# A two-layer recurrent-memory transformer on one core: the instruction order planned anew, one unit's product tied to VectorE, one row load released earlier

## The chip, the cores and the metric

The kernel runs on one core of one Trainium2 chip. The core has five engines that run side by side, each with its own queue of instructions: TensorE (PE, with its weight loads shown apart as PEld), VectorE (DVE), ScalarE (ACT), GpSimd (POOL) and SyncE (SP, which here only issues DMAs). The metric is the device time in microseconds of one execution. The times before are the median of three runs. The profile is of one further execution, whose own time is given beside its span.

## The reference

The input is one sequence of 2048 rows of 512 values in bf16. Two blocks, A and B, are applied twice, each on a normalised input and added back:

```python
    x = A_x
    x = x + _A_ref(_layernorm(x, axis=-1), A_mem0, A_Wq, A_Wk, A_Wv, A_Wo, A_seg_len)
    x = x + _B_ref(_layernorm(x, axis=-1), B_w1, B_w2)
    x = x + _A_ref(_layernorm(x, axis=-1), A_mem0, A_Wq, A_Wk, A_Wv, A_Wo, A_seg_len)
    x = x + _B_ref(_layernorm(x, axis=-1), B_w1, B_w2)
```

A is attention over segments of 32 rows with 8 memory rows in front, 32 heads of 128. The memory rows that a segment gives are the next segment's memory, so the 64 segments follow one another:

```python
        for s in range(n_seg):
            xs = x[:, s * seg_len:(s + 1) * seg_len, :].copy()
            h = jnp.concatenate([mem, xs], axis=1)
            q = jnp.einsum('btd,dhe->bhte', h, Wq)
            k = jnp.einsum('btd,dhe->bhte', h, Wk)
            v = jnp.einsum('btd,dhe->bhte', h, Wv)
            scores = jnp.einsum('bhqe,bhke->bhqk', q, k) * scale
            scores = jnp.where(mask[None, None], scores, -1000000000.0)
            p = _softmax(scores, axis=-1)
            o = jnp.einsum('bhqk,bhke->bhqe', p, v)
            o = jnp.einsum('bhte,hed->btd', o, Wo)
            mem = o[:, :M, :].copy()
            outs.append(o[:, M:, :])
```

B is a dense layer, relu(x w1) w2 with an inner width of 1376. The weights of A and of B are the same in both applications.

## The kernel before

The work goes in 66 steps. Step k handles segment k of the first application and segment k-2 of the second one together ("two layers" a = 0 and 1, 40 columns each: 32 rows and 8 memory rows). Steps 0 and 1 have the first layer alone, steps 64 and 65 the second alone. All weights stay in SBUF.

One step consists of these operations, whose names also stand in the planning tables:

- `queries_keys`: q and k projections from HT (the transposed 40 + 40 columns), 16 matmuls for four heads, copied out of PSUM to qT and kT by ACT or DVE.
- `values.mm.0` to `.3`: the value projection, copied to vw; some DMAs then place parts of vw in V0 (`place_values`, on SP).
- five units, `u0` to `u4`. Units 0 and 1 (`BLOCKED`) and unit 2 have eight heads, units 3 and 4 four heads. For each: `scores.mm` on TensorE; then on DVE `block` (adds the mask), `top` (maximum), `sub`; `exp` on ACT; on DVE `total` and `recip`; then `mul`. In units 0 and 1 `mul` and a 32-by-32 transpose (`turn`) are on DVE, and four copies, `stay` and `shift` for two halves, on ACT or POOL bring the result to PT. In units 2 to 4 `mul` may be on POOL or DVE, `turn` is on TensorE, and two masked copies (`keep`) bring it to PM.
- `attend`: probabilities times values, copied to OT by ACT or DVE (`attend.ev`).
- `project.mm.0` to `.4`: the output product from OT, one for each unit, accumulated in one PSUM bank (`st`). From it `project.ev` copies the new memory columns into the next step's HT (this is the recurrence: the next step's projections wait for it) and `project.rows` the others to OX.
- `finish`: OX is transposed by a DMA on SP (`finish.turn`), added to x on DVE (`add`), normalised over halves (`layernorm_halves`, "da"), turned on TensorE (`turned.turn.da`), and goes through the dense layer (`dense_layer.mm.da.0` to `.5`, with `relu` on ACT or DVE). The sum with the dense result (`total_x`) is normalised again ("db": `stats`, `swap`, `aggr` on DVE or ACT, `rstd.power` on POOL, `norm` on DVE), turned (`turned.turn.db`) and copied to the second layer's columns of the HT of the step after next. POOL also does `narrow`, `carry` (for the rows to be stored and the next x) and `widen` (the rows of the step after next from bf16 to f32).
- every fourth step `load_group` loads the next 128 rows by SP (`xb`, L919), normalises them ("dl") and turns them by a DMA.
- in steps 5 to 54 `late_values` computes value rows for later groups, one or two products a step.

The first 57 us load the weights (Wv, Wq, Wk, Wo on POOL's queue, w1 and w2 on SP's), spin TensorE on zeros, and compute value rows for seven row groups (`*values.mmg1.0` and so on).

Nothing of the order stands in the code as such. Class `Plan` collects all operations with their reads and writes, an engine or a choice of two engines, and a cost in microseconds for each. `order` then places them one after another in a planned time: on TensorE in the order of `PLACE` (a number for each product and phase of the run, plus `PERIOD` for each step), on other engines by a priority that follows from the operations that come after, shifted by the table `AHEAD`; `LOOK` is how far it looks past the earliest start. Where an operation may run on two engines, it is given to the one that ends it earlier in the planned time. `PAIRED` names products that take over the 64-column mode of the product before them. The instructions are then issued in the order of their planned starts, each engine's queue in that order. So a cost that is changed in the code changes nothing in an instruction itself, but can change the order on all engines and the engine of an operation.

Lines to know: L742 all 128-column and 64-column products by `across`, L1029 and L1031 copies by ACT and by DVE, L1035 and L1037 those of units 0 and 1 by ACT and by POOL, L1223 `sub`, L1226 `exp`, L1229 `total`, L1248 `mul` of units 2 to 4, L796 `norm` over halves, L765 statistics of whole rows, L747 and L752 the two parts of `rstd.power`, L919 the load of xb, L562 and L567 the loads of w1 and w2, L965 the transpose of OX.

Of the kernel before, what the change touches and what calls it, by code (L numbers as in the profile page):

```python
# [30 lines left out]
LOOK = 0.1074729  # L31
PERIOD = 26.155362
PLACE = {
# [421 lines left out]
def kernel(  # L455
# [21 lines left out]
    L = M + SEG  # L477
# [18 lines left out]
    plan = Plan()  # L496
# [994 lines left out]
```

## Time and profile before

| | us |
|---|---|
| median of three runs | 1590.68 (1589.81 to 1591.3) |
| time of the profiled execution | 1592.36 |
| its span | 1590.6 |
| start to the end of step 0's output products | 57.07 |
| step 1 | 25.71 |
| step 2 | 25.17 |
| step 3 | 25.08 |
| steps 4 to 63, each | 22.9 to 24.1 |
| step 63's end to the end of the span | 47.96 |

The mean granted clock of TensorE is 0.997 of full speed over the span. The chain of waits, which follows the work back from the last instruction, gives 90% of the span to TensorE, 3% to ScalarE, 2% to VectorE and 1% each to GpSimd and to DMAs. GpSimd waits 408.5 us for VectorE's second normalisation statistics (L793) in 64 waits, and VectorE 292.5 us for the DMA transpose of OX in 65 waits; both have little else to do at that point of a step. In the table of waits TensorE's own longest entries are small, 3.8 us for the copies to HT in 13 waits and 3.0 us for copies of hT in two.

In a timeline, a row is one instruction or several equal ones (xN), with its start and its length, and in brackets how long its engine had stood idle and what ended that. A matmul's length is from its issue to its modelled end, about 0.2 us, while matmuls follow each other at 0.036 us (128 columns, 80 rows).

### The profile page before, as it was taken

To read this page: it belongs to the slowest core of one execution; us is meant where nothing else is said; L and a number is where in the kernel's file an instruction comes from. 1 tells how busy PE (TensorE), PEld (TensorE's weight loads), DVE (VectorE), ACT (ScalarE), POOL (GpSimd) and SP (SyncE) were. 2 spreads that over 40 slices of the span, in tenths; PEclk is the share of its full clock that TensorE was granted. 3 is DMA by queue.
4 is the path that set the end of the run, shared out by engine and by line. 5 is a ranking of instruction groups with operands and counts; after the bars stand their busy time and mean duration, and the time that the engine had idled before them with its cause. 6 is when DMAs were issued, how large, how long until landed. Compare 5 with 4: busy or idle time off the path is not lost.

```text
span 1590.6 us, 101922 instructions
## 1 busy us (share of the span) xinstructions
PE 1566.3 (98%) x45454; PEld 1403.1 (88%) x45454; DVE 1024.2 (64%) x3237; ACT 1177.5 (74%) x3189; POOL 516.1 (32%) x1384
## 2 busy tenths in 40 slices
PE   8999999999999999999999999999999999999998
PEld 5688899889989989988988998999898998898887
DVE  4566766766765766676676576666667567667665
ACT  4567777777777777777777777777777777777775
POOL 5133323323323322332332333333233233233221
PEclk9999999999999999999999999999999999999999
DMA  9711111111011111111111111111011111110100
GB/s 371 241 38 26 26 27 32 28 25 40 21 37 28 31 28 24 29 33 34 26 33 23 33 25 38 34 24 35 21 31 28 27 32 26 26 26 21 25 17 8
DMA packets 67080, 66.74 MB, mean 42 GB/s; under 512 B 43496, under 2 KB 52944, under 8 KB 66640
## 3 DMA queue, kind: packets, MB, share of 16 engines
q1 hardware_dynamic: 60624, 39.89, 11.3%
q0 software_dynamic: 4992, 19.40, 3.2%
q8 instruction: 356, 5.83, 1.6%
q10 hardware_dynamic: 1024, 0.93, 0.2%
q14 instruction: 84, 0.69, 0.2%
HBM read 31.53 MB, written 9.96 MB: 26 GB/s over the span
## 4 chain that ended last, share of the span: by engine, by line
PE 90%; ACT 3%; DVE 2%; issue 1%; POOL 1%; DMA 1%; SPq 0%; POOLq 0%; DVEq 0%; ACTq 0%
PE work L742 36%; PE st L742 19%; PE fill L1101 16%; PE fill L742 7%; PE work L1332 5%; PE fill L864 5%; PE work L1190 3%; ACT PT L1035 1%; ACT es L1226 1%; DMA V<-vw 1%; ACT kT L1029 0%; DMA xb<-in_A_x_dram 0%; DVE es L1223 0%; ACT hT L852 0%; DVE mx L1213 0%
## 5 line engine op out<-in xcount | busy, mean ns | idle before, releaser
L742 PE MATMUL work<-HT,Wq_sb 128*128 128x80 bf16 (+2 forms) x10400 | 373.1, 201 | 3.9 <-ACT HT L1029 3.5
L742 PE MATMUL work<-HT,Wk_sb 128*128 128x80 bf16 (+2 forms) x10400 | 362.4, 201 | 0.7 <-ACT HT L1029 0.4
L742 PEld LDWEIGHTS <-Wq_sb 128*128 128x128 bf16 (+1 forms) x10400 | 334.2, 104 | 22.8 <-issue 5.7
L742 PE MATMUL st<-OT,Wo_sb 128*128 128x80 bf16 (+1 forms) x8448 | 344.6, 201 | 0.2 <-ACT OT L1029 0.2
L742 PEld LDWEIGHTS <-Wk_sb 128*128 128x128 bf16 (+1 forms) x10400 | 328.7, 104 | 14.2 <-issue 1.2
L742 PEld LDWEIGHTS <-Wo_sb 128*128 128x128 bf16 x8448 | 319.5, 99 | 16.3 <-issue 13.3
L1101 PE MATMUL fill<-Wv_sb,HT 128*64 128x512 bf16 x2112 | 274.7, 382 | 3.3 <-ACT hT L852 3.0
L1037 POOL COPY PT<-es 32x32 f32<-32x32 f32 (+4 forms) x521 | 156.1, 300 | 350.7 <-PE work L1190 164.3
L1029 ACT CAST qT<-work 128x320 bf16<-128x320 f32 (+1 forms) x452 | 188.8, 418 | 82.4 <-PE work L742 50.0
L1029 ACT CAST kT<-work 128x320 bf16<-128x320 f32 (+1 forms) x479 | 199.1, 416 | 42.9 <-PE work L742 4.5
L1029 ACT CAST vw<-fill 128x512 bf16<-128x512 f32 x258 | 151.2, 586 | 90.6 <-PE fill L1101 88.1
L747 POOL TENSOR_SCALAR ln<-ln 128x1 f32<-128x1 f32 x159 | 35.4, 223 | 524.2 <-DVE ln L793 408.5
L1029 ACT CAST OT<-work 128x320 bf16<-128x320 f32 (+1 forms) x399 | 152.6, 418 | 40.4 <-PE work L1332 39.3
L1270 ACT ACTIVATE PM<-work,half 128x160 bf16<-128x160 f32 (+2 forms) x317 | 133.8, 442 | 34.1 <-PE work L742 32.2
L1101 PEld LDWEIGHTS <-HT 128*64 128x64 bf16 x2112 | 101.5, 111 | 63.3 <-issue 4.8
L1223 DVE TENSOR_TENSOR es<-es,mx 128x320 f32<-128x320 f32 (+2 forms) x330 | 150.8, 469 | 1.8
L1226 ACT ACTIVATE es<-es 128x320 f32<-128x320 f32 (+2 forms) x330 | 130.3, 410 | 25.1 <-DVE es L1223 21.4
L1229 DVE TENSOR_REDUCE sm<-es 128x8 f32<-128x320 f32 (+2 forms) x330 | 128.5, 402 | 30.4 <-ACT es L1226 29.6
L1213 DVE TENSOR_REDUCE mx<-es 128x8 f32<-128x320 f32 (+2 forms) x330 | 127.6, 399 | 0.3
L742 PE MATMUL fill<-xnM,w_sb 128*128 128x64 bf16 (+1 forms) x3668 | 119.3, 194 | 0.7 <-ACT xnM L1029 0.5
L1204 DVE TENSOR_TENSOR es<-work,maskb 128x320 f32<-128x320 f32 (+1 forms) x132 | 59.0, 476 | 94.2 <-PE work L1190 91.4
L1190 PEld LDWEIGHTS <-qT 128*40 128x40 bf16 x4096 | 83.5, 98 | 33.5 <-issue 1.1
(111 smaller groups left out, 2361.0 us busy)
## 6 DMA issues: line engine op xcount, KB each, us to landing
V<-vw SPq DMA_DIRECT2D x248, 48.0 KB
V<-vh SPq DMA_DIRECT2D x120, 64.0 KB
Wq_sb<-in_A_Wq_dram POOLq DMA_DIRECT2D x2, 2048.0 KB, 23.0
Wk_sb<-in_A_Wk_dram POOLq DMA_DIRECT2D x2, 2048.0 KB, 28.1
Wo_sb<-in_A_Wo_dram POOLq DMA_DIRECT2D x2, 2048.0 KB, 39.9
vh<-vg SPq DMA_DIRECT2D x32, 128.0 KB
xb<-in_A_x_dram SPq DMA_DIRECT2D x16, 128.0 KB
Wv_sb<-in_A_Wv_dram POOLq DMA_DIRECT2D x1, 2048.0 KB, 13.3
```

Of the source, the lines that this page charges most:

```text
L742: nc.tensor.matmul(out_[u:v, :], lhsT=lhsT[:, u:v], rhs=rhs, start=start, stop=stop, tile_position=(0, u), **more)
L864: nc.tensor.matmul(yp[64 * u:64 * u + 64, 0:256], lhsT=hT[:, fc, :], rhs=w2_sb[:, fc, :].rearrange("p (j u d) -> p u j d", j=2, u=2)[:, u, ...
L1029: nc.scalar.copy(out=out_, in_=in_)
L1037: nc.gpsimd.tensor_copy(out=out_, in_=in_)
L1101: nc.tensor.matmul(vp[64 * b:64 * b + 64, :], lhsT=cols(c4), rhs=Wv_sb[:, c4, n * 512:(n + 1) * 512], start=(c4 == 0), stop=(c4 == NC4 - 1 ...
L1190: nc.tensor.matmul(v[64 * t:64 * t + L, a, i, s, :], lhsT=qT[:, hi, a * L:(a + 1) * L], rhs=kT[:, hi, a * L:(a + 1) * L], start=True, stop ...
L1213: nc.vector.tensor_reduce(out=by_head(mx), in_=e_rows(), axis=AX.X, op=ALU.max)
L1223: nc.vector.tensor_tensor(out=e_spread(), in0=e_spread(), op=ALU.subtract, in1=i1)
L1226: nc.scalar.activation(out=es[:, A], in_=es[:, A], func=ACTF.Exp, scale=SCALE)
L1229: nc.vector.tensor_reduce(out=by_head(sm), in_=e_rows(), axis=AX.X, op=ALU.add)
L1270: nc.scalar.activation(out=o, in_=i, func=ACTF.Copy, scale=half[:, b:b + 1])
L1332: nc.tensor.matmul(o[u:u + cols, :, a, :], lhsT=V[:, p, e0 + u:e0 + u + cols], rhs=spread(a, i, h2), start=True, stop=True, tile_position= ...
```

## The change

The two planning tables, `PAIRED` and `LOOK` are replaced (some 300 numbers; four lines of each are shown), and these costs and rules with them. `PERIOD` stays.

```diff
-LOOK = 0.1074729
+LOOK = 0.1164413
 PERIOD = 26.155362
 PLACE = {
-    ("*turned.turng0.0", 2): 113.397, ("*turned.turng1.0", 2): 114.607, ("*turned.turng2.0", 2): 122.366,
...
 PAIRED = {
-    ("project.mm.1", 0), ("project.mm.2", 0), ("project.mm.2", 4), ("project.mm.4", 0), ("project.mm.4", 4),
...
+    ("project.mm.1", 0), ("project.mm.2", 0), ("project.mm.3", 0), ("project.mm.4", 0), ("queries_keys.mmu0.0", 0),
...
 AHEAD = {
-    ("*layernorm.aggr", 1): -3.303, ("*layernorm.norm", 1): 34862.154, ("*layernorm.stats", 1): -2.846,
...
+    ("*layernorm.aggr", 1): -7.952, ("*layernorm.stats", 1): -189070.642, ("*make_mask", 1): 4.661,
...
 def t_moved(eng, n):
-    return 0.205 + 0.86e-3 * n if eng == ACT else 0.20 + 1.08e-3 * n
+    return 0.25 + 0.86e-3 * n if eng == ACT else 0.19 + 1.08e-3 * n
...
-            plan.op(POOL, 0.95, power, r=["half"], w=[ln])
+            plan.op(POOL, 0.82, power, r=["half"], w=[ln])
...
-        plan.op((ACT, DVE), (0.2, 0.2), swap, w=[ln])
+        plan.op((ACT, DVE), (0.30, 0.26), swap, w=[ln])
...
-        plan.op(DVE, 0.26, norm, r=[ln, *keys], w=[xn])
+        plan.op(DVE, 0.32, norm, r=[ln, *keys], w=[xn])
...
-        plan.op(SP, 0.78, load, r=[("taken", 4 * g - 4), ("out", 4 * g - 4)], w=[xb], lag=2.45)
+        plan.op(SP, 0.78, load, r=[("taken", 4 * g - 4), *([("out", 4 * g - 4)] if g > 1 else [])], w=[xb], lag=2.45)
...
-            plan.op(POOL, 2 * t_copy(256), carry, r=[("z", 0)], w=[keys[1]])
+            plan.op(POOL, 0.92, carry, r=[("z", 0)], w=[keys[1]])
...
-                plan.op(POOL, t_copy(256), narrow, r=[("z", 1)], w=[ob])
+                plan.op(POOL, 0.45, narrow, r=[("z", 1)], w=[ob])
...
-            def mul(eng):
+            def mul(eng=DVE):
...
-            plan.op((POOL, DVE), (t_pool(n), t_dve(n)), mul, r=[es, sm], w=where)
+            plan.op(*(((POOL, DVE), (t_pool(n), t_dve(n))) if n <= 160 else (DVE, t_dve(n))), mul, r=[es, sm], w=where)
...
-            plan.op((ACT, POOL), (t_moved(ACT, L * nj), t_moved(POOL, L * nj) + 0.07), stay, r=[es, PT], w=[(PT, b)])
+            plan.op((ACT, POOL), (t_moved(ACT, L * nj), t_moved(POOL, L * nj)), stay, r=[es, PT], w=[(PT, b)])
```

Two of these edits change what may be done, beside the order. `mul` of the third unit (`u2`, n = 320 in steps with both layers) can no longer go to POOL. The load of the first further row group (`load_group` with g = 1, in step 1) no longer waits for step 0's transpose of OX on SP (`("out", 0)`); it still waits for step 0's memory copy (`("taken", 0)`).

What the built programs show of the order: both have the same 10,822 planned operations. In a steady step the order on TensorE is, before and after (an excerpt from the first scores to the end of the step; pairs of `qk` stand for `queries_keys`, `da` for the dense layer, `sc` for scores, `at` for attend, `pr` for the output product):

```
before: sc1 sc0 qk2.2 v2 qk2.0 qk2.1 turn.da v1 qk2.3 v3 sc2 qk3.0 da0 qk3.1 qk4.0 qk4.1 da1 sc3 da2 sc4
        at1 at0 da3 da4 turn2 da5 pr0 turn3 at2 pr1 at3 turn4 pr2 at4 pr3 turn.db pr4
after:  sc0 sc1 qk2.0 qk2.2 v0 v1 qk2.1 qk2.3 v3 sc2 turn.da qk4.0 qk3.0 da0 qk3.1 da1 qk4.1 sc3 da2 at0
        sc4 at1 da3 turn2 da4 da5 pr0 turn3 at2 pr1 turn4 at3 pr2 at4 pr3 turn.db pr4
```

The DVE order of step 30, from unit 3's reciprocal on, and POOL's from unit 2's product on:

```
DVE  before: recip3 total_x stats.db total4 recip4 aggr.db mul4 keep3.1 norm.db at.ev3.0
     after:  recip3 total_x total4 stats.db recip4 mul4 keep3.1 swap.db aggr.db at.ev3.0 norm.db
POOL before: mul2 mul3 narrow carry rstd.db widen
     after:  mul3 narrow carry widen rstd.db
```

Engines of operations that have a choice, over the run, where many moved:

| operation | before | after |
|---|---|---|
| `scores.mul` | DVE 207, POOL 123 | DVE 267, POOL 63 |
| `layernorm_halves.swap.db` | DVE 4, ACT 60 | DVE 64 |
| `dense_layer.relu` | ACT 195, DVE 3 | ACT 148, DVE 50 |
| `queries_keys.ev` | ACT 931, DVE 125 | ACT 975, DVE 81 |
| `scores.stay` and `shift` | ACT 201, POOL 327 | ACT 152, POOL 376 |
| `scores.keep` | DVE 79, ACT 317 | DVE 57, ACT 339 |

On SP the first lines change from "transpose of OX, four w1 loads, xb load, w2 loads, row transpose" to "xb load, transpose of OX, four w1 loads, row transpose, w2 loads". On POOL the mask and the second root stand ahead of the two Wo loads; before, they stood behind.

More of the change, by code (lines that the diff above doesn't have):

```diff
@@ new lines @@
+    ("*layernorm.aggr", 1): -7.952, ("*layernorm.stats", 1): -189070.642, ("*make_mask", 1): 4.661,
+    ("*prepare_more.zero_w2", 1): -41.906, ("*rstd.raise_", 1): -5.01, ("*turned.keep", 1): 140461.982,
+    ("*turned.turn", 1): 130.17, ("attend.ev", 0): 0.205, ("attend.ev", 2): 0.149, ("attend.mm", 0): -141847.173,
+    ("attend.mm", 1): 93388.877, ("bulk.land", 1): 0.047, ("dense_layer.mm.da", 1): 0.081,
+    ("dense_layer.relu.da", 0): -75998.358, ("dense_layer.relu.da", 1): 3230.06, ("dense_layer.relu.da", 2): -0.052,
@@ new lines @@
+    ("early_store.put", 1): -49649.171, ("finish.add", 0): -35230.884, ("finish.add", 1): -12100.287,
+    ("finish.add", 2): -64.499, ("finish.narrow.db", 0): -1.52, ("finish.store.da", 2): -13.443,
+    ("finish.store.db", 0): -0.123, ("finish.total_out.da", 2): -90151.838, ("finish.total_x.da", 0): -0.024,
+    ("finish.total_x.da", 1): 0.284, ("finish.turn", 2): 33.797, ("finish.turn_near", 2): 3.087,
+    ("finish.widen", 0): 1.436, ("finish.widen", 1): 10.067, ("get_x", 1): -54690.148, ("late_values.ev", 0): -3.113,
@@ new lines @@
+    ("layernorm_halves.norm.da", 2): 0.151, ("layernorm_halves.norm.db", 0): 2.128,
+    ("layernorm_halves.norm.db", 1): -0.915, ("layernorm_halves.stats.da", 0): 13687.157,
+    ("layernorm_halves.stats.da", 1): 0.323, ("layernorm_halves.stats.da", 2): -84750.62,
+    ("layernorm_halves.stats.db", 0): -2.938, ("layernorm_halves.stats.db", 1): 1.326,
+    ("layernorm_halves.swap.da", 0): -56685.136, ("layernorm_halves.swap.da", 1): 0.655,
+    ("layernorm_halves.swap.da", 2): 36.788, ("layernorm_halves.swap.db", 0): 0.227,
@@ new lines @@
+    ("layernorm_halves.swap.db", 1): 131238.655, ("load_group.load.dl", 0): -3.193, ("load_group.load.dl", 1): -2.217,
+    ("load_group.turn_far.dl", 1): 0.841, ("load_weights.dma", 1): -23604.969, ("place_values.dma", 1): -1.747,
+    ("prep_x.cp", 0): -0.338, ("prep_x.cp", 1): -3.672, ("prepare.first_exp", 1): -19.747, ("prepare.keep", 1): 8.604,
+    ("prepare.place", 1): 53401.671, ("prepare.turn", 1): 2.221, ("prepare.zero", 1): -1354.661,
+    ("prepare.zero_last", 1): -98887.921, ("prepare.zero_none", 1): -1.096, ("prepare_late.load", 0): -92232.192,
@@ new lines @@
+    ("project.ev", 0): 0.174, ("project.ev", 1): 0.154, ("project.ev", 2): -1.945, ("project.first", 1): -69.357,
+    ("project.mm", 0): 10.274, ("project.mm", 1): 133742.033, ("project.mm", 2): 65.416,
+    ("project.rows", 0): -2766.799, ("project.rows", 1): 7.099, ("queries_keys.ev", 0): 15.868,
+    ("queries_keys.ev", 2): -103526.145, ("queries_keys.mm", 0): -70335.54, ("queries_keys.mm", 2): -1.989,
+    ("rstd.power.da", 0): 1.301, ("rstd.power.da", 1): 143.283, ("rstd.power.da", 2): -9.528,
@@ new lines @@
+    ("rstd.power.db", 0): -21571.742, ("rstd.power.dl", 1): 0.41, ("scores.block", 0): 0.227,
+    ("scores.block", 1): 1.135, ("scores.block", 2): 42546.547, ("scores.exp", 1): 3.968, ("scores.exp", 2): -22.937,
+    ("scores.keep", 1): 120278.391, ("scores.mm", 0): 0.965, ("scores.mm", 1): -0.13, ("scores.mm", 2): 53469.948,
+    ("scores.mul", 0): 112.91, ("scores.mul", 1): 0.096, ("scores.mul", 2): 12.538, ("scores.recip", 1): 52381.849,
+    ("scores.recip", 2): -3.712, ("scores.shift", 1): 28746.395, ("scores.shift", 2): 20526.276,
@@ new lines @@
+    ("scores.stay", 0): -2299.032, ("scores.stay", 2): -40540.573, ("scores.sub", 0): -37.08,
+    ("scores.sub", 1): -32755.82, ("scores.sub", 2): 1.716, ("scores.top", 0): 27715.681, ("scores.total", 1): 97.858,
+    ("scores.total", 2): 208136.995, ("scores.turn", 1): -53625.561, ("scores.turn", 2): 0.246,
+    ("turned.keep", 0): 2.548, ("turned.keep.da", 1): 44.635, ("turned.keep.da", 2): 144612.281,
+    ("turned.keep.db", 1): 185440.58, ("turned.turn", 0): -38648.799, ("turned.turn.da", 0): -75405.957,
@@ L204 @@
+    ("turned.turn.da", 2): 0.583, ("turned.turn.db", 0): -73377.416, ("values.ev", 0): 0.441, ("values.ev", 1): 0.01,
+    ("values.ev", 2): -59.755, ("values.mm", 0): -25.052, ("values.mm", 1): 35.335, ("values.mm", 2): 0.371,
+    ("zero_columns.zero", 1): -12272.977,
 }
```

54 lines of the change are left out of this document (6 added, 48 removed), and 230 rows, old and new, of tables (PAIRED, PLACE).

## The prediction

> **What bounds the kernel now.** The busy table comes first, then the stages cut at the last output product of steps 0, 1, 2, 3 and 63.
>
> ```profile
> PE 1566.3 (98%) x45454; PEld 1403.1 (88%) x45454; DVE 1024.2 (64%) x3237; ACT 1177.5 (74%) x3189; POOL 516.1 (32%) x1384
> ```
> ```profile
> 0.00:57.07 57.07, 50.95 (x801) 33.15 (x802) 26.52 (x90) 29.40 (x70) 24.10 (x63) 0.94 0.93 351
> 57.07:82.78 25.71, 21.99 (x560) 17.38 (x560) 14.18 (x57) 13.29 (x44) 7.24 (x20) 1.00 0.59 168
> ...
> 133.03:1542.64 1409.61, 1403.60 (x41564) 1273.31 (x41564) 924.16 (x2883) 1073.27 (x2889) 461.67 (x1236) 1.00 0.13 28
> ```
>
> Columns: stretch, length, busy time of PE, PEld, DVE, ACT, POOL, granted clock, DMA share, GB/s. TensorE bounds every stage, so only time in which it waits can be won. Its busy time hides short waits, because a matmul counts 0.2 us from issue to end while the next follows after 0.036 us. I therefore took, from the trace, the time from each planned product's first matmul to that of the next one, and its excess over the shortest tenth of the same product in steps 3 to 62. These excesses add up to 28 us, and 0.47 us of them in each of the nine steps from 55 on is the step's own round trip (last output product, copy, next projection). An ordinary step loses about 0.27 us: 0.08 ahead of unit 1's attend, 0.03 ahead of unit 3's turn, 0.15 ahead of the fourth output product. A step that normalises a row group (every fourth) loses about 0.45. The largest single wait is in step 1, in the chain of waits and in the timelines of DVE and PE:
>
> ```profile
> 61.70 6.23 DMA xb<-in_A_x_dram
> ```
> ```profile
> 67.94 0.69 DVE L765 BATCH_NORM_STATS2 ln<-xb 128x6 f32<-128x512 bf16 x1 [3.33 <-DMA xb<-in_A_x_dram]
> ```
> ```profile
> 71.48 1.05 PE L1101 MATMUL fill<-Wv_sb,HT 128*64 128x512 bf16 x8 [2.85 <-ACT hT L852]
> ```
>
> The row load leaves SP at 61.70, behind four weight loads (58.62 to 61.64). VectorE stands 3.33 us at its statistics, with the scores' totals queued behind them, and TensorE stands 2.85 us for the work that comes of these.
>
> Last, one ordinary step (30, whose first score product is at 749.96; times "+" count from there):
>
> ```profile
> 760.32 0.66 DVE L1223 TENSOR_TENSOR es<-es,mx 128x160 f32<-128x160 f32 x1
> ...
> 761.75 0.31 DVE L1223 TENSOR_TENSOR es<-es,mx 128x160 f32<-128x160 f32 x1
> ...
> 765.04 0.57 DVE L796 TENSOR_SCALAR xr<-vx,ln 128x256 bf16<-128x256 f32 x1 [0.85 <-POOL ln L752]
> 765.53 0.48 DVE L1031 CAST OT<-work 128x320 bf16<-128x320 f32 x1
> ```
> ```profile
> 760.07 0.72 POOL L1248 TENSOR_TENSOR P<-es,sm 128x320 bf16<-128x320 f32 x1 [0.55 <-ACT hT L852]
> 762.29 0.45 POOL L1248 TENSOR_TENSOR P<-es,sm 128x160 bf16<-128x160 f32 x1 [1.50 <-ACT PM L1270]
> ```
> ```profile
> 765.88 0.20 PE L1332 MATMUL work<-PM,vw 128*128 128x80 bf16 x1
> 766.06 0.73 PE L742 MATMUL st<-OT,Wo_sb 128*128 128x80 bf16 x16
> ```
>
> VectorE is full from +0.5 to +14. The same subtraction takes 0.31 alone and 0.66 while GpSimd multiplies. Unit 3's copy to OT stands behind a normalisation that waits 0.85 for GpSimd, and the fourth output product starts late for it (766.06).
>
> **The change, part by part.** In the changed program each steady step has the same TensorE products, the same four switches between 128 and 64 columns (0.096 each), only in another order; so TensorE's work there is unchanged and the sum is one of waits.
>
> *Steady step, worked with the rows of step 30.* DVE: unit 0's block at +0.47; two blocks, tops, subtractions at 0.40 each; normalisation; totals from +3.36 (subtraction ends 2.56, exp 2.69 to 3.16); both products and transposes end at +6.62; unit 2's subtraction at +7.51. Its exp follows on ACT at +8.14 to 8.60 (before: 8.64 to 9.10, behind three more copies), so its total starts at +8.64, 0.5 earlier. Now the third unit's product stands on DVE: 61 POOL products of 0.725 go, and 61 come to DVE. The nearest row is the one such product DVE ran before (0.493); bounds 0.44 (start to start) and 0.73. I take 0.44. In return unit 3's subtraction takes 0.31, not 0.66, and one PSUM copy fewer (0.46) stands between. A relu (the 256-column one that DVE ran took 0.43) falls into a wait for a projection. Reciprocal of unit 3 comes out at +11.95 to 12.10, against 12.02 to 12.19, POOL's product at 12.25 to 12.70, against TensorE's need at +12.82: the 0.03 may go. Unit 4's product ends at +13.9, needed at +14.33. Unit 0's attend at +9.51 needs copies that are done by +8; unit 1's at +9.9 needs a bank freed by unit 3's block at +9.8: the 0.08 goes. Unit 3's copy to OT now precedes the normalisation: DVE +14.85 to 15.3, needed at +15.83: the 0.15 goes. So 0.22 of 0.27, in 44 steps: -9.7 (bounds 0 and -11.9).
>
> *Steps with a row group.* The statistics (0.69) and the normalisation (0.40) still stand in DVE's chain: unit 3's turn comes at +13.05 against 12.82, unit 1's attend about 0.1 late. 0.45 becomes 0.25, 15 steps: -3.0 (bounds +1.5 and -6.8). Two steps stood 0.78 and 0.40 for a late row transpose (first at 1152.20); the product that waits now stands 2.6 us later in its step: -1.0.
>
> *What gets worse.* POOL's widen (0.83) now stands ahead of the second normalisation's root in 59 steps; it stood behind. And the pair of swap copies moved from ACT (60 of 64) to DVE (0.34), behind unit 4's product. DVE: aggregate ends +14.73. POOL: product to 12.70, narrow 0.40, carry 0.89, widen 0.83 end at +14.95; root 0.88 to +15.85; normalisation 0.41, no longer slowed to 0.57 by widen, to +16.29; turn possible at +16.4, and TensorE is there at +16.40. The second of before had 1.0 us to spare; this has none. In 20 steps a late value product (0.44) now stands right ahead and covers it. I take 0.06 in 40 steps: +2.5 (bounds 0 and 0.45 each, +18).
>
> *Other moved evacuations* (relu, swap, stay and shift pieces, OT copies): ACT loses net 97 operations, DVE gains 108, both inside the sums above; the cover is the slack given there.
>
> *Start.* The early rows' first turn still waits for POOL's first root (ends 7.21) behind the same transfers. After it four value products stand ahead of the second turn; two waits of before, 1.08 us at 10.07 and 0.73 at 18.13, are filled. The first product that needs the second Wv transfer (landed at 16.2 by the trace's DMA events, as the other landings here) started at 18.87, and could start at 16.4 to 17.0. The mask (2.6 us of POOL) moves ahead of the second root; this ends at 10.95 instead of 10.75, needed after 12.7. A cap: the third output product needs the last Wo transfer, landed at 50.5; it started at 55.02. So 0 to -4.3; I take -3.0. One value product (0.87) moves from step 0 into step 1, which cancels.
>
> *The row load.* It stands ahead of the output transpose on SP, can leave at about the step's start and lands while DVE waits for that transpose anyway (5.94 us idle there): -2.8 (bounds 0 and -3.7, the whole idle time of this stage). The transpose, and the four weight loads behind it, leave 0.46 later; the dense layer's turn stands nine products later in the step, which covers it (uncovered: 0.46). The second weights move behind the row transpose; they landed at 75.2 at the latest and are needed some 3 us earlier than before: bound +1. Steps 2, 3 and the tail: 0 (bounds -1.5 and +1.5).
>
> Cost constants, LOOK and the planning tables act through the order alone.
>
> Sum: -9.7 - 3.0 - 1.0 + 2.5 - 3.0 - 2.8 = -17.0. The profiled execution took 1592.36 (span 1590.6 and 1.8 around it), so 1575.4; it lies 1.7 above the median 1590.68. The forecast, as a median, is 1573.7, or **1574**.
>
> [...]
>
> **Rivals.**
> *The root comes late (slower).* One mechanism: widen ahead of the root on POOL. Unit 3's product, carry or widen each stretch when DVE is active (copies of the same shape spread from 0.31 to 0.46, the carry halves from 0.39 to 0.46). If the root starts 0.5 later than worked out, the turn stands in some 40 uncovered steps: 20 us in place of 2.5, which makes 1591; at 0.7 it is 1599. It decides from 0.49 on (19.5 over 40). For: no slack is left. Against: widen now leaves the normalisation unslowed, and the root itself stretched in few cases (0.567 median, 0.570 at the ninth tenth).
> *Waits only move.* DVE's chain is held by POOL once a step, 0.35 as the subtraction was; unit 3's and unit 4's turns then stand as long as the waits removed, and the steady gain (11.2) is gone: 1585. For: six POOL copies of units 0 and 1 now follow one another. Against: POOL's longest instruction leaves.
> *The early load is hidden anyway*: the transpose or the weights behind it hold step 1 in its place: 1576.5; with the start's gain lost too, 1580.
> *More than the forecast*: all steady waits but the round trips go (24), and the start reaches its caps (8): about 1559.
>
> **Chances.** Forecast 0.50; root late 0.20; waits only move 0.14; load hidden 0.08; more 0.08. A measurement of this kernel tells about 0.2% (3.2 us) from no change. Faster: 0.50 + 0.08 + 0.08 and 0.08 of the waits that move, 0.74; within 0.2%: the rest of these 0.06 and 0.02 of the late root, 0.08; slower: 0.18. Range 1562 to 1598, from near the lowest bound to the late root at 0.7; its own range, without the rivals, is 1565 to 1584.
>
> **What would show it.** In step 1 the statistics of xb with no DMA wait, and no TensorE gap over 1 us. In a steady step: OT's DVE copy ahead of the normalisation; no gap ahead of the fourth output product; unit 3's subtraction at 0.31; steps of 23.1 in place of 23.33. Wrong: gaps ahead of the second normalisation's turn (TensorE waiting for xr), or ahead of the turns of units 3 and 4.

## The result, and the profile after

The changed kernel takes 1577.05 us (median of 4 runs, 1576.44 to 1580.34), beside 1590.99 for the kernel before (median of 4): a ratio of 0.9917, interval 0.9900 to 0.9935, so 0.65 to 1.0% faster. The slowest of the four, 1580.34, had a mean granted clock of 0.997, the other three 1.0. The forecast was 1574. The profiled executions, against which the sum was made, took 1592.36 and 1576.44: 15.9 less, where the sum said 17.0. A later series gave 1576.58 (e11 below).

The busy table of the changed kernel, then the stages cut, as before, at the last output product of steps 0, 1, 2, 3 and 63 (stretch, length, busy time of PE, PEld, DVE, ACT, POOL, granted clock, DMA share, GB/s):

```profile
PE 1553.5 (99%) x45393; PEld 1389.3 (88%) x45393; DVE 1074.4 (68%) x3406; ACT 1126.3 (72%) x3011; POOL 479.8 (30%) x1393
```
```profile
0.00:54.13 54.13, 48.28 (x789) 32.44 (x789) 26.57 (x89) 28.63 (x68) 25.72 (x68) 1.00 0.98 370
54.13:80.04 25.91, 23.32 (x571) 17.77 (x568) 13.47 (x55) 14.15 (x46) 5.86 (x17) 1.00 0.60 186
...
105.23:128.93 23.70, 23.04 (x691) 20.85 (x692) 17.68 (x54) 16.78 (x46) 7.60 (x22) 1.00 0.09 21
128.93:1526.46 1397.53, 1392.77 (x41564) 1261.55 (x41564) 972.73 (x3045) 1024.91 (x2727) 424.69 (x1236) 1.00 0.13 29
```

TensorE still bounds every stage, and the same number of matmuls in steps 4 to 63 (41,564) takes 12.1 us less. Stage by stage, in us:

| stage | before | after | difference | the sum said |
|---|---|---|---|---|
| step 0 | 57.07 | 54.13 | -2.9 | -3.9 (-3.0, and the product that moves out) |
| step 1 | 25.71 | 25.91 | +0.2 | -1.9 (-2.8, and that product) |
| steps 2 and 3 | 50.25 | 48.89 | -1.4 | 0 |
| steps 4 to 63 | 1409.6 | 1397.5 | -12.1 | -11.2 |
| behind step 63 | 48.0 | 48.2 | +0.3 | 0 |

Step 0 differs in one thing that the sum did not use: its granted clock (the share of TensorE's full speed), 0.94 before and 1.00 after. The same stretch of both kernels, first before, then after:

```profile
8.27:15.10 6.83, 5.79 (x35) 2.64 (x36) 3.13 (x11) 2.13 (x4) 6.21 (x22) 0.50 1.03 399
8.27:15.10 6.83, 5.78 (x55) 3.18 (x55) 2.40 (x7) 3.37 (x7) 6.28 (x18) 1.00 1.03 397
```

In the kernel before the granted clock is 0.5 in these 6.83 us, and TensorE does 35 matmuls in the busy time in which it does 55 after. A value product (eight matmuls of 512 columns) takes 1.71 us there and 0.86 at the full clock. The matmuls bear out the 1.00 of the changed kernel from about 10.4 on; up to there it runs slower too (its 14 matmuls of 256 columns from 5.63 on start 0.21 us apart, those of the kernel before from 4.87 on 0.11). All four profiles with the order of before (before, e6, e7, e8) have such a stretch of 6.83 us, beginning between 8.3 and 10.5; of the ten with the new order none has one between 11.0 and the end of step 0.

The second table takes the waits apart by the measure of the prediction (first matmul of a product to the first of the next, over the shortest; here over the shortest of both kernels), summed over steps 3 to 62:

| wait ahead of | before | after |
|---|---|---|
| the fourth output product | 5.5 | 0.0 |
| unit 1's attend, behind unit 4's scores | 4.8 | 0.1 |
| what follows unit 1's attend (row-group steps) | 3.4 | 0.6 |
| what follows unit 3's turn | 1.9 | 0.2 |
| the fifth output product | 0.9 | 2.5 |
| the next step's projection (the round trip) | 4.4 | 4.8 |

One ordinary step shows it. Timeline of VectorE and POOL in step 32 of the changed kernel, whose first score product is at 788.39 (start, duration, what, and idle time before it with its releaser):

```profile
798.92 0.32 DVE L1218 TENSOR_TENSOR es<-es,mx 128x160 f32<-128x160 f32 x1
...
802.34 0.55 DVE L1026 COPY ln<-ln 64x6 f32<-64x6 f32 x2
802.93 0.21 DVE L788 BATCH_NORM_AGGREGATE ln<-ln 128x2 f32<-128x12 f32 x1
803.15 0.49 DVE L1026 CAST OT<-work 128x320 bf16<-128x320 f32 x1
804.21 0.41 DVE L791 TENSOR_SCALAR xr<-vx,ln 128x256 bf16<-128x256 f32 x1 [0.56 <-POOL ln L747]
```
```profile
800.96 0.40 POOL L1002 CAST xg<-vx 128x256 bf16<-128x256 f32 x1
801.42 0.83 POOL L997 COPY xg<-vx 32x256 f32<-32x256 f32 x2
802.30 0.85 POOL L948 CAST xg<-xb 32x256 f32<-32x256 bf16 x2
803.30 0.22 POOL L742 TENSOR_SCALAR ln<-ln 128x1 f32<-128x1 f32 x1
803.60 0.57 POOL L747 TENSOR_TENSOR ln<-ln,mhalf 128x1 f32<-128x1 f32 x1
```
```profile
804.24 0.74 PE L737 MATMUL st<-OT,Wo_sb 128*128 128x80 bf16 x16
804.81 0.22 PE L737 MATMUL fill<-ident,xr 128*128 128x64 bf16 x2
804.91 0.73 PE L737 MATMUL st<-OT,Wo_sb 128*128 128x80 bf16 x16
```

Unit 3's subtraction takes 0.32; its copy to OT (803.15) stands ahead of the normalisation, ends at 803.64, and the fourth output product follows at 804.24 with no wait. The second normalisation ends at 804.62 and its turn starts at 804.81, on time. In the 44 steps where this turn follows the fourth output product directly, with no late value product to cover it, 41 waited 0.00 for it. The normalisation's POOL chain (narrow, carry, widen, root) has no gap.

The start of step 1 has not gone the way the sum had it. SP of the kernel before, then SP and PE of the changed kernel:

```profile
62.16 7.16 SPq L567 DMA_DIRECT2D w_sb<-in_B_w_dram  x3
```
```profile
1.73 0.51 SPq L914 DMA_DIRECT2D xb<-in_A_x_dram  x1
...
63.80 1.20 SPq L922 DMA_TRANSPOSE xnA<-xr  x1
65.05 3.87 SPq L562 DMA_DIRECT2D w_sb<-in_B_w_dram  x3
```
```profile
52.69 1.51 PE L737 MATMUL st<-OT,Wo_sb 128*128 128x40 bf16 x54 [0.80 <-issue]
57.79 0.91 PE L737 MATMUL work<-HT,Wq_sb 128*128 128x40 bf16 x30 [0.85 <-issue]
75.53 0.75 PE L859 MATMUL fill<-w_sb,hT 128*64 128x256 bf16 x6 [0.97 <-DMA w_sb<-in_B_w_dram]
```

The row load leaves at 1.73, not at the start of step 1: it stands third on SP's queue, behind two loads issued at 0.79 and 1.27. The wait of 2.85 us for it is gone. In its place stand a wait for the second dense weights (0.97), whose loads now stand behind the row transpose (before, they stood ahead of it, which left at 70.54), and two waits for which the profile has no releaser, the first of them in step 0.

### The profile page after: what moved, and what is told of

Its sections match the earlier page's. It is cut to its first block, busy times and chain, and to the rows that moved or that the text cites. A ratio compares the mean times of both kernels' runs of the same rounds, so it can differ in the third digit from the quotient of the medians.

```text
span 1574.7 us, 101546 instructions
## 1 busy us (share of the span) xinstructions
PE 1553.5 (99%) x45393; PEld 1389.3 (88%) x45393; DVE 1074.4 (68%) x3406; ACT 1126.3 (72%) x3011; POOL 479.8 (30%) x1393
## 3 DMA queue, kind: packets, MB, share of 16 engines
q1 hardware_dynamic: 60624, 39.89, 11.2%
## 4 chain that ended last, share of the span: by engine, by line
PE 95%; DMA 2%; POOL 1%; DVE 1%; issue 1%; ACT 0%; SPq 0%; POOLq 0%; DVEq 0%
PE work L737 39%; PE st L737 18%; PE fill L1096 16%; PE fill L737 8%; PE fill L859 5%; PE work L1327 5%; PE work L1185 4%; DMA Wq_sb<-in_A_Wq_dram 1%; DMA w_sb<-in_B_w_dram 0%; POOL xg L997 0%; POOL xg L948 0%; ACT HT L1024 0%; POOL ln L747 0%; SPq L562 0%; DVE es L1218 0%
## 5 line engine op out<-in xcount | busy, mean ns | idle before, releaser
L737 PE MATMUL work<-HT,Wk_sb 128*128 128x80 bf16 (+2 forms) x10400 | 351.4, 201 | 0.4 <-ACT HT L1024 0.4
L737 PE MATMUL work<-HT,Wq_sb 128*128 128x80 bf16 (+2 forms) x10400 | 342.8, 201 | 5.7 <-ACT HT L1024 4.0
L737 PEld LDWEIGHTS <-Wq_sb 128*128 128x128 bf16 (+1 forms) x10400 | 317.4, 104 | 17.4 <-issue 7.9
L1032 POOL COPY PT<-es 32x128 f32<-32x128 f32 (+5 forms) x590 | 164.2, 278 | 405.9 <-DVE es L1286 288.3
L1024 ACT CAST qT<-work 128x320 bf16<-128x320 f32 (+1 forms) x513 | 214.6, 418 | 91.1 <-PE work L737 52.2
L1096 PE MATMUL fill<-Wv_sb,HT 128*64 128x512 bf16 x2112 | 263.3, 381 | 0.1
L1024 ACT CAST kT<-work 128x320 bf16<-128x320 f32 (+1 forms) x462 | 187.1, 422 | 49.3 <-PE work L737 11.0
L1024 ACT CAST vw<-fill 128x512 bf16<-128x512 f32 x259 | 144.4, 582 | 64.2 <-PE fill L1096 63.7
L1024 ACT CAST OT<-work 128x320 bf16<-128x320 f32 (+1 forms) x391 | 146.1, 426 | 47.2 <-PE work L1327 47.2
L1218 DVE TENSOR_TENSOR es<-es,mx 128x320 f32<-128x320 f32 (+2 forms) x330 | 136.6, 431 | 1.9
```

The lines of the kernel that those rows point to most:

```text
L737: nc.tensor.matmul(out_[u:v, :], lhsT=lhsT[:, u:v], rhs=rhs, start=start, stop=stop, tile_position=(0, u), **more)
L1024: nc.scalar.copy(out=out_, in_=in_)
L1032: nc.gpsimd.tensor_copy(out=out_, in_=in_)
L1096: nc.tensor.matmul(vp[64 * b:64 * b + 64, :], lhsT=cols(c4), rhs=Wv_sb[:, c4, n * 512:(n + 1) * 512], start=(c4 == 0), stop=(c4 == NC4 - 1 ...
L1218: nc.vector.tensor_tensor(out=e_spread(), in0=e_spread(), op=ALU.subtract, in1=i1)
```

## The experiments

e6 to e8 start from the kernel before, the others from the changed kernel. Where an operation is moved, it is moved in the planned list, after planning, by a helper `put(key, step, "ahead" or "behind", other key, other step)`; so nothing else changes place. The runs were made on four chips (e1 to e4, e5 to e8, e9 to e11, e12), on which the kernel before took 1591.6, 1591.6, 1592.6 and 1591.9; a difference between runs of two chips is sure to about 1 us only. Stage lengths are read from each kernel's trace. Steps 0 and 1 vary between executions of the same order (step 0 of the changed kernel ended between 53.4 and 54.1, that of the kernel before between 57.1 and 58.1), the steady steps hardly (1397.5 and 1397.9 in the two profiles of the changed kernel), so differences of about 1 us are read from the stage, not from the total.

### e1: is there slack behind the second root?

```diff
-                nc.gpsimd.tensor_copy(out=ob[:, :], in_=Z[:, :])
+                for _ in range(2):
+                    nc.gpsimd.tensor_copy(out=ob[:, :], in_=Z[:, :])
```

> The changed kernel with finish's narrow copy (0.40 us on POOL) done twice in each step that has it, 62 steps. On POOL narrow, carry, widen and the second normalisation's root follow one another without a gap (+12.56 to +15.78 in step 30), so the root starts 0.40 later. Forecast's theory (no slack is left behind the root; only a late value product right ahead covers it): the second normalisation's turn stands 0.40 longer in the some 40 steps that show 0.05 there now, and little in the others: +16 us, 1593 (range 1589 to 1600). Rival (the root still has slack, TensorE has other work at that point): under +3 us.

Measured: 1587.5 us, 0.9976 of before (0.9966 to 0.9985), 10.9 over e11. The weight loads of the turns from xr, in the groups by line (busy, mean ns of one, then idle time before them by releaser), first in the changed kernel, then here:

```profile
L737 PEld LDWEIGHTS <-xr 128*128 128x128 bf16 x182 | 12.2, 100 | 3.3 <-DVE xr L791 1.6 <-DVE xr L766 1.2
```
```profile
L737 PEld LDWEIGHTS <-xr 128*128 128x128 bf16 x182 | 11.4, 99 | 14.0 <-DVE xr L791 10.6 <-DVE xr L766 2.4
```

The wait for the normalisation grows by 9 us. Ahead of the second normalisation's turn stand 10.8 us instead of 0.1, 0.21 to 0.28 in 33 of the 44 uncovered steps. Of the 0.40 that was added, some 0.13 was slack; the result lies between the two theories. The mechanism of the first rival is real, and this kernel stands 0.13 us in front of it; but the 0.05 us per step that the trace of the changed kernel shows at the end of a step are not that wait.

### e2: widen behind the root

```diff
+        for k in range(1, STEPS - 2):
+            put("finish.widen.0", k + 2, "behind", "rstd.power.db.0", k)
```

> The changed kernel with POOL's widen put back behind the second normalisation's root in 61 steps, everything else in the planned order. Theory 1, as the prediction priced it (widen ahead holds the root): the 0.05 us ahead of the second normalisation's turn in 41 steps go, -2 us, 1575. Theory 2 (in the trace VectorE's aggregate ends at +14.74 and widen at +14.76 of step 30, the root starts at +14.91 for either): the root starts no earlier, and the normalisation runs beside widen again, 0.57 instead of 0.42, so the turn comes 0.1 to 0.15 later in some 40 steps: +4 to +6 us, 1581 to 1583.

Measured: 1574.81 (0.9897, 0.9883 to 0.9910); steps 2 to 63 are 0.8 shorter than in the changed kernel, the rest of the 1.8 to e11 lies within what the first steps vary. VectorE in step 32 (first score product at 787.26):

```profile
801.21 0.35 DVE L1026 COPY ln<-ln 64x6 f32<-64x6 f32 x2
801.59 0.21 DVE L788 BATCH_NORM_AGGREGATE ln<-ln 128x2 f32<-128x12 f32 x1
...
802.87 0.57 DVE L791 TENSOR_SCALAR xr<-vx,ln 128x256 bf16<-128x256 f32 x1 [0.36 <-POOL ln L747]
```

Neither theory. Without widen beside them the two swap copies take 0.35 instead of 0.55, so the root starts 0.2 earlier; the normalisation then runs beside widen and takes 0.57 instead of 0.41, and its end moves by only 0.05. The 0.05 us per step stay: they stand ahead of the fifth output product, which waits for unit 4's copy to OT. What was gained lies in steps 14, 27 and 39, where the root of a late row also stands behind widen: 0.36 of the 0.45 us that TensorE waits there for the late row's turn went.

### e3 and e4: the order on SP in step 1

e3 moves the second weights ahead of the row transpose, e4 the row load back to where it stood:

```diff
+        for i in (2, 1, 0):
+            put(f"load_dense.dma2.{i}", 0, "behind", "load_dense.dma1.3", 0)
```
```diff
+        put("load_group.load.dl.0", 1, "behind", "load_dense.dma1.3", 0)
```

> The changed kernel with the second weights' loads (four DMAs) put ahead of the row transpose on SP's queue in step 1. Theory 1: the wait of the dense layer's fifth product (0.97 us, released by the w_sb DMA) and the chain behind it (add, carry, widen, root, normalisation, turn at the end of step 1) come from their place behind the transpose, which waits for the normalised row group until 63.80, and the loads could leave at 58.8: the step gets 1.0 to 1.5 us shorter, 1575.7. Theory 2: the weights' space is free only later (the stores of the values that lie in it), or the transfers share the queues with the stores then, so they land no earlier: within 0.3 us, and the transpose leaves later instead.

> The changed kernel with the first row load put back behind the output transpose and the four loads of the first dense weights on SP, as it stood before; nothing else moved. Theory 1 (the forecast's): the load leaves at about 58.8 instead of at the start of the step and lands near 64, VectorE stands at its statistics with the scores queued behind, step 1 gets 2 to 3 us longer: 1579 to 1580. Theory 2 (hidden anyway: step 1 is held by the second weights' transfers and the code loading): under +0.8 us.

Measured: e3 1575.09 (0.9896, 0.9883 to 0.9910), step 1 takes 24.48 instead of 25.91, -1.43; the second weights left at 58.08. e4 1580.87 (0.9933, 0.9920 to 0.9945), step 1 takes 29.69, +3.8. SP and PE of e3, then VectorE and PE of e4:

```profile
58.08 1.93 SPq L562 DMA_DIRECT2D w_sb<-in_B_w_dram  x3
```
```profile
72.94 1.39 PE L859 MATMUL fill<-w_sb,hT 128*64 128x256 bf16 x22
```
```profile
63.28 0.69 DVE L760 BATCH_NORM_STATS2 ln<-xb 128x6 f32<-128x512 bf16 x1 [12.04 <-DMA xb<-in_A_x_dram]
```
```profile
68.42 0.27 PE L737 MATMUL fill<-ident,xr 128*128 128x128 bf16 x2 [3.41 <-ACT V L1024]
```

In e3 the products of the second dense weights run through (22 in one piece); their chain to the end of the step (sum, carry, widen, root, normalisation, turn) starts earlier by as much. In e4 the statistics are VectorE's next instruction and wait for the row load, and TensorE stands 3.41 us for what is queued behind them. Right behind this wait the granted clock is 0.5 from 68.65 to 72.06, so the 3.8 us are not those of the wait alone; and the second weights, which in e4 still stand behind the row transpose, are not waited for. So both theories on the early load held in part: it takes a wait away, and what it pushed back on SP costs 1.43.

### e5 and e7: the engine of the third unit's product

e5 gives the product back to POOL in the changed order; e7 gives it to VectorE in the order of before:

```diff
+            if o.kind == "scores.mul" and o.key.startswith("scores.mulu2") and 2 <= o.step < STEPS:
+                o.fn = lambda fn=o.fn: fn(POOL)
```
```diff
+            if o.kind == "scores.mul" and o.key.startswith("scores.mulu2"):
+                o.eng = DVE
```

> The changed kernel with the third unit's product back on POOL in 62 steps, at the same place of the planned order. Theory 1 (the order carries the gain, the engine of this product little): VectorE is freed of about 0.45 and loses 0.35 by the subtraction of unit 3, which runs beside POOL's product again (0.66 for 0.31), and POOL is idle there (+9.5 to +12.2 in a step): within 2 us of the changed kernel. Theory 2 (the product's engine carries the gain): unit 3's turn and what follows come 0.1 to 0.35 late in a step, +6 to +20 us.

> The kernel before with the third unit's product on VectorE in every step, the order as it was. Theory 1: VectorE gets 0.44 to 0.49 and saves 0.35 at unit 3's subtraction; POOL's later work starts with unit 3's product, which waits for VectorE, so its root comes no earlier: -1 to +5 us. Theory 2 (the engine of the product is what gains): unit 3's subtraction and all behind it come earlier, -5 to -10 us.

Measured: e5 1576.68 (0.9903, 0.9890 to 0.9917), 0.1 from e11; steps 4 to 63 take 1397.74. e7 1594.19, 1.0017 of before (1.0008 to 1.0026): slower by 2.6, of which 0.8 in steps 4 to 63. POOL and VectorE of e5 in step 32, at the same place as above:

```profile
797.99 0.72 POOL L1243 TENSOR_TENSOR P<-es,sm 128x320 bf16<-128x320 f32 x1
```
```profile
798.91 0.32 DVE L1218 TENSOR_TENSOR es<-es,mx 128x160 f32<-128x160 f32 x1
```

In the new order unit 3's subtraction starts at 798.9 whichever engine has the product, and POOL's product has ended by then (798.71), so the two no longer meet. What VectorE does ahead of that subtraction (the block of unit 4) waits for unit 4's scores, which TensorE ends at 798.55; the product fills time that is idle without it. In the old order (e7) it does not: the waits around unit 3's turn grow from 1.9 to 4.4 us. The restriction by itself brings nothing; the order does.

### e6: the copy to OT ahead of the normalisation, alone

```diff
+        for k in range(DELTA, STEPS):
+            if find("attend.evu3.0", k).eng == DVE:
+                put("attend.evu3.0", k, "ahead", "layernorm_halves.norm.db.0", k - 1)
```

> The kernel before with one thing moved: VectorE's copy of unit 3 to OT ahead of the second normalisation, in the 58 steps in which it stands behind. Theory 1 (the forecast's largest steady term): the 0.15 us ahead of the fourth output product go; some 0.05 may come back at the fifth, whose copy of unit 4 is then the last: -4 to -6 us. Rival (waits only move: the normalisation comes later by the copy, 0.1 to 0.2, and the second normalisation's turn stands for it): within 1.5 us.

Measured: 1588.21, 0.9977 of before (0.9969 to 0.9986), -3.4. VectorE and PE in step 32 (first score product at 798.23):

```profile
813.02 0.49 DVE L1031 CAST OT<-work 128x320 bf16<-128x320 f32 x1 [0.56 <-PE work L1332]
813.43 0.45 DVE L796 TENSOR_SCALAR xr<-vx,ln 128x256 bf16<-128x256 f32 x1
```
```profile
814.18 0.74 PE L742 MATMUL st<-OT,Wo_sb 128*128 128x80 bf16 x16
814.75 0.22 PE L742 MATMUL fill<-ident,xr 128*128 128x64 bf16 x2
```

The 5.5 us ahead of the fourth output product fall to 0.0, and 2.1 us come up ahead of the fifth: 0.05 per step, the same as in the changed kernel. Steps 4 to 63 are 4.7 shorter by the trace. One swap of two VectorE operations gives between a quarter and two fifths of the change's steady gain.

### e8: the early row load alone, in the kernel before

```diff
+        put("load_group.load.dl.0", 1, "ahead", "finish.turn.0", 0)
```

> The kernel before with the first row load put ahead of the output transpose on SP's queue, and nothing else moved. Theory 1 (the forecast's): VectorE's wait of 3.33 us at the statistics and TensorE's of 2.85 us in step 1 go, and what stands behind costs under 0.5: step 1 gets 2.3 to 2.9 us shorter. Rival (something else is late next, the second weights or the instruction loads): under 1 us.

Measured: 1589.35, 0.9986 (0.9977 to 0.9995), -2.2; step 1 takes 23.95 instead of 25.71 in the profile of before, -1.8. The granted clock is 1.00 in that step in both. (In e7 and e6, whose step 1 has the order of before, it takes 26.6 and 27.5; there the granted clock is 0.5 for 3.4 and 6.8 us of it.) PE of e8:

```profile
68.38 0.55 PE L742 MATMUL fill<-xnM,w_sb 128*128 128x64 bf16 x13 [1.15 <-DMA w_sb<-in_B_w_dram]
```

The wait of 2.85 is gone; the first dense weights, awaited 0.16 before, are now awaited 1.15. So theory 1 holds for the wait, and the rival for part of the gain.

### e9 to e12: the waits without a releaser, and the moves together

```diff
+        put("*values.mmg6.3", 0, "ahead", "project.mm.2", 0)
+        put("*values.mmg6.1", 0, "behind", "queries_keys.mmu0.1", 1)
```

> The changed kernel with two of the early value products (0.87 us each, eight 512-column matmuls) moved forward: one from behind the last output product of step 0 to ahead of its third, one from the middle of step 1 to behind the second projection there. TensorE stands 0.95 in that third output product (51.7) and 1.0 at the sixth projection of step 1 (56.7), with no releaser in the profile, 1.5 us after a 16 KB transfer on the instruction queue began (50.27, 55.34). Theory 1 (TensorE waits for its instructions, because 40-column matmuls use them up faster than they come; a long product in between hides it): both waits go, step 0 and 1 end 1.5 to 1.9 us earlier, 1575.4. Theory 2 (it waits for the last output weights' transfer or something else at a fixed time): the waits only change place, under 0.5 us.

> The changed kernel with four moves together: the second weights' loads ahead of the row transpose (e3: step 1 shorter by 1.43), widen behind the second root (e2: steps 2 to 63 shorter by 0.8), the two value products of e9 moved forward (1.5 to 1.9 by its theory 1, else 0), and in steps 5 and 30 the late rows' turn and its copy ahead of the third output product (a late value product waits 0.63 us for them in both: 1.2). If they add up: 5 us by theory 1 of e9, 3.4 by theory 2, so 1572 to 1573.6.

> The changed kernel once more, as it is, beside the other two on the same chip: 1576.4 to 1577.5. In the runs so far the end of step 0 moved between 53.4 and 54.1 with no change to step 0; this shows how much of a difference under 1 us the start alone can make.

> The kernel of e10 without the two value products moved forward: the second weights' loads early, widen behind the root, the late rows' turn early. In e10 a new wait of 1.22 us with no releaser stood at 69.89, 2.4 us after an instruction transfer began at 67.45; in e3 with the same early loads but the products in their old places none stood there. If that wait came of the place of the products against the instruction transfers, step 1 ends about 78.2 here, 1.5 us earlier than in e10, and the gains of e2, e3 and the turn (0.8, 1.43, 1.2) add up to 3.4 under the changed kernel of the same day: 1572.8 to 1573.2. If the early loads themselves delay the instructions, the wait comes back and it stays at 1574.2 or above.

e10 has the edits of e2, e3, e9 and this one; e12 the same without e9's:

```diff
+        for k in (3, 28):
+            put("turned.turnr1.0", k, "ahead", "project.mm.2", k + 2)
+            put("turned.keepr1.0", k, "ahead", "attend.evu4.0", k + 2)
```

| run | time | ratio to before, interval | step 1 ends at | steps 4 to 63 |
|---|---|---|---|---|
| e11, changed kernel | 1576.58 | 0.9898, 0.9884 to 0.9913 | 79.53 | 1397.93 |
| e9 | 1575.45 | 0.9891, 0.9877 to 0.9906 | 78.67 | 1397.84 |
| e10 | 1574.22 | 0.9884, 0.9867 to 0.9900 | 79.81 | 1395.64 |
| e12 | 1572.36 | 0.9880, 0.9864 to 0.9897 | 78.75 | 1395.70 |

PE of e9, then of e10:

```profile
57.28 1.11 PE L737 MATMUL work<-HT,Wq_sb 128*128 128x40 bf16 x38 [0.42 <-issue]
```
```profile
69.89 0.27 PE L737 MATMUL work<-HT,Wk_sb 128*128 128x40 bf16 x4 [1.22 <-issue]
```

In e9 the wait of 0.80 in step 0's third output product is no longer in the view and the one in step 1 falls from 0.85 to 0.42: a long product moved ahead of both places takes most of the waiting away, as theory 1 has it (that TensorE waits there for its instructions is not shown directly, for no view names a releaser); step 1 ends 0.9 to 1.4 earlier, less than the 1.5 to 1.9 expected, for the next step's first projection now waits for its input (0.27). The place speaks for theory 1 too: in every profile of the new order, e9's too, the wait in step 1 stands behind the same number of matmuls, 863 from the start, though the product there is another in e9. In e10 the sum failed: a wait of 1.22 appears behind 1119 matmuls, and right behind it the granted clock is 0.5 from 71.36 to 74.78. e12, without e9's moves, waits 0.25 at the same matmul, and is the fastest of all: its four runs (1571.89 to 1573.42) lie below the four of e11 (1576.24 to 1577.0). The medians are 4.2 us (0.27%) apart, on two chips; the profiled spans, 1571.1 and 1574.6, are 3.5 apart, of which 2.2 in steps 4 to 63. Why the wait is 1.22 in e10 and 0.25 in e12 is not shown.

## Why the prediction was right, and where it was not

*Ordinary steps, -9.7.* Right in place and nearly in size: an ordinary step takes 23.12 instead of 23.33. The copy to OT is shown by e6 (5.5 us went, as the changed order has it). The wait ahead of unit 1's attend is gone by the trace (4.8 to 0.1); no run moved it alone, so its reason is argued.

*The product on VectorE.* "I take 0.44" for the product and 0.31 for the subtraction were both right as durations (0.40 from start to start in step 32, and 0.32). That they would pay for each other was not needed: e5 shows the same time with the product on POOL.

*Row-group steps, -3.0, and late transposes, -1.0.* By the trace 2.8 went behind unit 1's attend in row-group steps, and 1.7 at the four late transposes (0.78, 0.40 and two of 0.28; the prediction had counted only the first two).

*The root, +2.5.* Here the number nearly came out and the reason did not (0.06 in 40 steps is 2.4, too). The trace shows 2.5 us at the end of the steps, mostly as 0.05 in 41 of them (0.9 of it stood there before), but e2 and e6 show it ahead of the fifth output product, for unit 4's copy. For the root TensorE waits nothing in an ordinary step; it has 0.13 to spare (e1). The step "this has none" was off by these 0.13; in three steps with a late row's root, which the prediction did not look at, TensorE waits 0.45 each for that row's turn, and 0.36 of it is widen's (e2).

*Start, -3.0.* The size came out and the reason did not, so this was luck. In the two profiled executions step 0 is 2.9 shorter, of which 0.87 is the product that moved out. Between the means of the profiles with either order (57.7 for four, 53.7 for eight) it is 4.0, so 3.1 without the product. The sum had two waits filled. But TensorE's idle time in step 0 hardly fell (57.07 less 50.95 is 6.12 before, 54.13 less 48.28 is 5.85 after), and up to the second Wv transfer it still stands three times for about half a microsecond (0.49, 0.55 and 0.55 before; 0.46, 0.58 and 0.55 after). What fell is the time of the matmuls themselves: at the granted clock of 0.5 the early value products took 2.5 to 2.8 us more than at the full clock in the four profiles with the old order, and 0.2 to 1.0 in the ten with the new one. The step that failed is the one that took the granted clock for settled, although the shown row has 0.94. In the new order 14 of the 24 early matmuls on zeros run from 5.63 on, where TensorE idled before (5.80 to 7.71). Whether they keep the clock up is not shown: no run moved them alone.

*The row load, -2.8.* This is the term that failed, and most of the difference between sum and result. The wait itself went, as forecast. But "the second weights move behind the row transpose" was taken at 0, with a bound of +1, and costs 1.43 (e3). What holds them is not their place by itself: the transpose waits for the normalised rows until 63.80, and they, behind it on SP's queue, left at 65.05, when its 1.20 us were over; in e3, ahead of it, they left at 58.08. The two waits without a releaser (0.80 in step 0, 0.85 in step 1) were not in the sum; e9 shows that they change with the order (the kernel before has two of them, 0.85 and 0.22, in step 0). In step 1 that makes -2.85 for the wait, +0.87 for the product that moved in, +1.43 and +0.85, together +0.3; measured is +0.2. The load also left 50 us earlier than "about the step's start": the planner's condition puts it in a list and is no wait on the chip.

*Step 3, taken at 0.* It is 1.4 shorter: the waits of before behind the first output product (0.81), unit 0's attend (0.25) and unit 2's turn (0.19) are gone; the late rows' copy, awaited 0.35 in step 5 before, is awaited 0.63 in steps 5 and 30.

*The rivals.* The late root exists as a mechanism: the turn waits as soon as the root is 0.13 later, and 0.40 (e1) cost 10.9 in all. Waits that only move: 2.1 of 5.5 did (e6). The load hidden anyway: in part, by the transfers behind it (1.43 of some 2.9). That VectorE is slower beside work of POOL is in the traces: the subtraction of unit 3's shape takes 465 ns on average before and 315 after, and e2 shows it of widen, beside which the swap copies take 0.55 instead of 0.35 or, with widen behind the root, the normalisation 0.57 instead of 0.41. The product now on VectorE took 0.48 in each of its 62. On POOL, over steps 4 to 63, carry's halves took 0.39 to 0.47 before (two up to 0.57) and 0.39 to 0.40 after, widen's 0.39 to 0.40 and 0.39 to 0.43, and unit 3's product 0.45 in every step of either kernel, so of a stretching of that product nothing is seen.

## What to carry to other kernels

When a load moves forward on a queue, price what comes to stand behind a waiting entry there; the gain of the load was certain, and up to half of it went to the transfers behind it (1.43 of 2.9, and in e8 1.0 of 2.9). Of several edits that come with a new order, undo each alone inside the new order and do each alone in the old one: the one that looked like the cause (an engine's exclusive product) was worth nothing, and one swap of two instructions a quarter or more. A wait of the predicted size is no proof of the predicted cause; stretch the suspected chain by a known amount and see how much of it arrives. And where a stage gets shorter, look at its granted clock before its waits are given the credit (0.94 and 1.00 in step 0).

## What the runs showed of the hardware

Waits of TensorE with no releaser, of 0.2 to 1.4 us, stand behind the same numbers of matmuls in all profiles, whatever product is there: behind 351 and 607 in the four with the old order, behind 735, 863 or 1119 in those with the new one. These places are 128 or 256 matmuls apart, with as many weight loads beside them. The changed kernel's trace has 355 pieces of 16 KB on the instruction queue and 45,393 matmuls, one piece to about 128. A piece takes about 1 us (at 50.27 and 55.34 in the changed kernel), in the steady steps too (0.9 to 1.5). But 128 matmuls of 40 columns, 25 ns apart, are over in 3.2 us, of 80 columns, 36 ns apart, in 4.6, and of 512 columns, 108 ns apart, in 13.8. The waits moved or went when only the order of long and short products changed (e9, and e10 beside e12). From this the author takes it that TensorE waits for its instructions at these places; no view shows it directly. In the steady steps, with 36 ns matmuls, no such wait of 0.1 us is seen. Those seen are in the first two steps; of the 128 matmuls ahead of each, 78 to 120 have 40 columns in the kernel before and the changed one. Whether the bulk transfers that run beside those steps lengthen the waits is not shown.

The granted clock of TensorE was lower behind some waits of 1.2 to 3.4 us and not behind others. It is 0.5 for 3.41 or 6.83 us behind waits of 1.22 (e10), 1.40 (e1), 1.92 (the kernel before, at 7.71) and 3.41 (e4). Behind the 2.85 of step 1 of the kernel before it stays at 1.00, so the length of the wait alone does not decide.

Two copies of 64 by 6 values each took 0.55 us together beside a cast on POOL (widen) and 0.35 without it; over the steady steps of the changed kernel the medians are 0.54 in 59 pairs and 0.35 in 61. So copies as small as these, too, were slower beside it.
